# The first chunk's residual accumulated in PSUM by TensorE, its sums copied out by ScalarE

## The chip, the cores and the metric

The kernel runs on one core of one Trainium2 chip. The metric is the device time of one execution in microseconds (us). All times below are of this core; "layer 0" and "layer 1" are the two passes that the program makes over the same pair of stages.

## The reference, cut to what matters

```python
def _A_ref(x, w_r, w_i):                       # spectral filter
    X = rfft2(x.astype(float32), axes=(-2, -1)) * (w_r + 1j * w_i)
    return irfft2(X, s=(S, D)).astype(bfloat16)

def _B_ref(x, w1, b1, w2):                     # dense layer with mish
    h = x @ w1 + b1
    return (h * tanh(softplus(h))) @ w2

x = A_x                                        # bf16, 2048 rows of 1024
for _ in range(2):
    x = x + _A_ref(layernorm(x), A_w_r, A_w_i)
    x = x + _B_ref(layernorm(x), B_w1, B_b1, B_w2)     # F = 3584
```

The place of the change is the seam between the two lines of the loop body: the inverse transform's last step gives sums, the old x is added to them (the residual), each row is normalised (mean and variance over its 1024 values), and the normalised rows enter the first dense product.

## The kernel before, in words

The activations `XS` stay in the on-chip memory SBUF as 16 tiles of 128 rows by 1024 columns. The program is a straight list: every engine (TensorE or PE, VectorE or DVE, ScalarE or ACT, GpSimd or POOL, SyncE or SP) executes its own instructions strictly in the order in which the Python code emits them. Buffers are `Res` objects; an instruction waits for the semaphores of the last writers and readers of what it touches. The accumulator memory PSUM has eight banks of 512 fp32 columns, each with its own `Res`. A matmul group that writes a bank which TensorE itself wrote last waits for TensorE's own semaphore.

`layer_A` is the spectral filter. Its last transform step needs `UT`, which goes through DRAM and comes back by DMA in four quarters (`u_last`). While these are under way, TensorE runs `spin(26, 0)` (L629): 26 matmuls of 512 columns whose results nobody reads, written to bank 0.

`layer_B` begins with that last step, `i4` (L951): for a column l of 128, one matmul with `UT[:, l, :]` as the weights gives sums for some of the 16 tiles. The rows are handled in chunks of four tiles. Chunk 0 (tiles 0 to 3) comes first, in four quarters u of 32 columns of l, quarter u in banks 2u and 2u+1. Per quarter, VectorE adds the sums of tiles 0 and 1 to `XS` in place (L973), ScalarE copies those of tiles 2 and 3 into a staging buffer `YC` (L549), and VectorE takes statistics of the fresh quarter of tiles 0 and 1 (`stats_quarter`, L471, L473). The other twelve tiles are made by `rest(bank, n)`: n columns of l, n matmuls of 96 columns, copied into the staging buffer `YS` by ScalarE, or by VectorE where `dve` is given. In all 128 columns are needed, in pieces of 15, 13 or 10; a piece in bank 3 uses banks 3 to 5, one of ten in bank 6 uses banks 6 and 7.

Then `root` (square root on ScalarE L431, reciprocal on VectorE L433) and `apply` (L511) normalise tiles 0 and 1, `spin(6, 7)` runs, `transposed` turns them by eight TensorE transposes each (L1007) into banks 6 and 7, VectorE copies these out (L1012), and `mm1(chunk, fg, half)` (L1041) is the first dense product, for half a chunk (256 columns) or a whole one (512). ScalarE applies mish (L1045), after a table load (`warm`, L424). Tiles 2 and 3 are added from `YC` (L1117), given statistics (`stats_dve`, L459, L462), scales (L489 to L502) and `apply`, and are turned in the middle of `mm1(0, 3, 0)`.

The order around the change is written out by hand:

```python
for u in range(4):                    # i4, add and copy, stats of quarter u
    ...
rest(0)
self.root(0, 2)
rest(3)
...
for fg in range(4):
    mm1(0, fg, 0, mid=turns(0, 2, 3) if fg == 3 else ())
    rest(3)
    if fg == 2:
        rest(6, 10, dve)
mm1(0, 0, 1)
rest(3, 13)
```

The DMAs of the first weights (`load_w1`) are issued by SP once all of `UT` has landed.

Of the kernel before, what the change touches and what calls it, by code (L numbers as in the profile page):

```python
# [6 lines left out]
ALU = mybir.AluOpType  # L7
P = 128
# [171 lines left out]
class KB:  # L180
# [487 lines left out]
    def layer_A(self, li):  # L668
# [7 lines left out]
        dve, act, sp, pool = self.dve, self.act, self.sp, self.pool  # L676
# [146 lines left out]
        def u_turn(g, half):  # L823

            u = U[g % 3]
            if g == 7:
                h = slice(8 * half, 8 * half + 8)
                if half == 0:
                    u_back(6)
                self.dma(act, self.u_d[g][:, h, :], u.ap[:, h, :], f"uwh{half}", reads=[u.res], writes=[self.r_ud7[half]])  # L830
                if half:
                    u_last()
            elif half:
                self.dma(sp, self.u_d[g], u.ap, f"uw{g % 3}", reads=[u.res], writes=[self.r_ud[g]])
                if g:
                    u_back(g - 1)
# [28 lines left out]
        for stage, g, h in self.order_A():  # L865
# [19 lines left out]
            else:  # L885
                i2(g, h)
                u_turn(g, h)
        self.spin(26, 0)
        if li == 0:
            self.op(self.pool, lambda e: e.tensor_copy(self.B1[:], self.B1h[:]), reads=[self.r_b1h], writes=[self.r_b1])  # L890
        self.w1_buf = [self.alloc(f"W1_{i}", (self.W1_OFF + i * 4096, 140 * K + (i - 4) * 4096)[i > 3], [8, 256]) for i in range(6)]
# [48 lines left out]
    def keep_filter(self, g):  # L940

        i = 2 * g % 8
        self.dma(self.pool, self.w_d[g], self.wt_pair(i), f"ws{g % 4}", reads=[w.res for w in self.WT[i:i + 2]], writes=[self.r_wd[g]])

    def i4(self, lo, nb, u0, n, bank):

        w = 8 * nb
        k = 512 // w
        fns = []
        for l in range(n):  # L950
            fns.append(lambda e, l=l: e.matmul(self.PS[:, bank + l // k, l % k * w:(l % k + 1) * w], self.UT.ap[:, u0 + l, :],  # L951
                                               self.MT[:, 8 * lo:8 * lo + w], start=True, stop=True))
        self.group(fns, reads=self.r_ut[u0 // 32:(u0 + n - 1) // 32 + 1] + [self.r_mt], writes=self.r_bank[bank:bank - (-n // k)])

    def i4_out(self, lo, nb, u0, n, bank, staged=None, prog=None, tiles=None):

        w = 8 * nb
        k = 512 // w
        t0, tn = tiles or (0, nb)

        for b0, m, i in ((0, n // k, k), (n // k, 1, n % k)):
            if not m or not i:
                continue
            src = self.PS[:, bank + b0:bank + b0 + m, 0:i * w].rearrange("p b (i c) -> p c b i", c=w)[:, 8 * t0:8 * (t0 + tn)]
            l = slice(u0 + b0 * k, u0 + b0 * k + m * i)
            rb = self.r_bank[bank + b0:bank + b0 + m]

            def at(ap):
                return ap.rearrange("p n (h l) -> p (n h) l", l=P)[:, :, l].rearrange("p c (b i) -> p c b i", i=i)
            if staged is None:  # L970
                j = slice(lo + t0, lo + t0 + tn)
                xs = at(self.XS[:, j, :])
                self.op(self.dve, lambda e, src=src, xs=xs: e.tensor_tensor(xs, src, xs, ALU.add), reads=rb, parts=self.r_xs[j])  # L973
            else:

                self.copy(prog or self.act, at(staged.ap), src, [], rb, parts=[staged.res])


    def load_w1(self, after=()):
# [7 lines left out]
    def layer_B(self, li, last):  # L987
        pe, dve, act, sp, pool = self.pe, self.dve, self.act, self.sp, self.pool
# [5 lines left out]
        def transposed(c, t, xn, eng=None):  # L994
            bank = 6 + nt[0] % 2
            nt[0] += 1
            xn.unread = False
            if t == 0:
                if XT[c % 2] is None:
                    off = self.ob[f"XT{c % 2}"]  # L1000
                    XT[c % 2] = self.alloc(f"XT{c % 2}", off, [8, 512])
                    r_xt[c % 2] = self.sub_res(XT[c % 2], f"xt{c % 2}h", 2, off, 8192)
                for r in r_xt[c % 2]:
                    r.begin()
            fns = []
            for db in range(8):
                fns.append(lambda e, db=db: e.transpose(PSb[:, bank, db * P:(db + 1) * P], xn.ap[:, db * P:(db + 1) * P],  # L1007
                                                        self.IDENT[:]))
            self.group(fns, reads=[xn.res, self.r_ident], writes=[self.r_bank[bank]])
            dst = XT[c % 2].ap[:, :, t * P:(t + 1) * P]  # L1010
            src = PSb[:, bank, :].rearrange("p (a b) -> p a b", b=P)
            fn = (lambda e: e.activation(dst, src, ACT.Copy)) if eng is act else (lambda e: e.tensor_copy(dst, src))  # L1012
            self.op(eng or dve, fn, reads=[self.r_bank[bank]], parts=[r_xt[c % 2][t // 2]])
# [12 lines left out]
        def mm1(c, fg, half=None, mid=()):  # L1026
            n = base + 14 * (c // 2) + fg
            wb = self.w1_buf[n % 6]
            x = XT[c % 2]
            tok = slice(0, 512) if half is None else slice(256 * half, 256 * half + 256)  # L1030
            w = tok.stop - tok.start
            for fl in range(2):
                if fl:
                    for f in mid:
                        f()
                ft = 2 * fg + fl
                bank = nh[0] % 3
                nh[0] += 1
                fns = []
                for db in range(8):  # L1040
                    fns.append(lambda e, db=db, bank=bank, fl=fl: e.matmul(  # L1041
                        PS[:, bank, 0:w], wb.ap[:, db, fl * P:(fl + 1) * P], x.ap[:, db, tok], start=(db == 0), stop=(db == 7)))
                self.group(fns, reads=[wb.res] + (r_xt[c % 2] if half is None else [r_xt[c % 2][half]]), writes=[self.r_bank[bank]])
                at, ra = AT[c % 2], r_at[c % 2][ft]
                self.op(act, lambda e, bank=bank, ft=ft: e.activation(at.ap[:, ft, tok], PS[:, bank, 0:w], ACT.Mish,  # L1045
                                                                      bias=self.B1[:, ft:ft + 1]),
                        reads=[self.r_bank[bank], self.r_b1], writes=[ra])
            if c % 2 and half != 0 and self.w1_next == n + 6 and n + 6 < base + 28:
                self.load_w1()
# [41 lines left out]

        YS = self.alloc("YS", self.o["YS"], [12, self.D])
        YS.res.begin()
        YC = self.alloc("YC", self.ob["XT1"], [2, self.D])
        YC.res.begin()
        xn = {}
        for j in range(2):
            self.r_xs[j].begin()

        def at_tiles(c):  # L1100
            off = self.ob[f"AT{c}"]
            AT[c] = self.alloc(f"AT{c}", off, [NF, 512])
            r_at[c] = [Res(f"AT{c}_{ft}") for ft in range(NF)]
            for ft, r in enumerate(r_at[c]):
                r.inherit(AT[c].res)
                self.live.append((off + ft * 1024, off + ft * 1024 + 1024, r))

        def rest(bank, n=15, prog=act):

            u0 = self.u0  # L1110
            self.u0 += n
            self.i4(4, 12, u0, n, bank)
            self.i4_out(4, 12, u0, n, bank, staged=YS, prog=prog)

        def residual(j):
            y, i = (YS, j - 4) if j > 3 else (YC, j - 2)
            self.op(dve, lambda e: e.tensor_tensor(self.XS[:, j, :], self.XS[:, j, :], y.ap[:, i, :], ALU.add),  # L1117
                    reads=[y.res], writes=[self.r_xs[j]])

        def turns(c, *ts):  # L1120
            return [lambda t=t: transposed(c, t, xn[4 * c + t]) for t in ts]

        self.u0 = 0


        for u in range(4):
            self.i4(0, 4, 32 * u, 32, 2 * u)
            self.i4_out(0, 4, 32 * u, 32, 2 * u, tiles=(0, 2))
            self.i4_out(0, 4, 32 * u, 32, 2 * u, staged=YC, tiles=(2, 2))
            for j in range(2):  # L1130
                self.stats_quarter(j, u)
        rest(0)
        self.root(0, 2)
        rest(3)
        for j in range(2):
            xn[j] = self.apply(j)
        self.spin(6, 7)
        for j in range(2):
            transposed(0, j, xn[j])
        rest(3)  # L1140
        self.warm(ACT.Mish)
        at_tiles(0)
        for j in (2, 3):
            residual(j)
            self.stats_dve(j)
        self.scales(2, 2)
        for j in (2, 3):
            xn[j] = self.apply(j)
        for fg in range(4):
            mm1(0, fg, 0, mid=turns(0, 2, 3) if fg == 3 else ())  # L1150
            rest(3)
            if fg == 2:
                rest(6, 10, dve)
        mm1(0, 0, 1)
        rest(3, 13)
        assert self.u0 == P
        for j in range(4, 8):
            residual(j)
# [105 lines left out]
```

## Time and profile before

| what | value |
|---|---|
| median of 3 runs | 1017.17 us (1016.41 to 1017.61) |
| profiled execution, its own time | 1017.47 us |
| span of that execution, first to last instruction | 1015.7 us |
| TensorE busy | 959.8 us, 94% |
| VectorE busy | 327.2 us, 32% |
| ScalarE busy | 346.8 us, 34% |
| granted TensorE clock | 1.000 |

The seam of layer 0 lies at 109 to 140 us of the span, that of layer 1 at 600 to 632 us. A TensorE "busy" counts each matmul from its start to its modelled end; as matmuls are pipelined, the step from one to the next is shorter than the duration of one. For sums of TensorE work the step is used: 448 matmuls of 512 columns take 96.69 us in the chain of work, which is 0.2158 us each, and 16 of 256 columns take 1.75 us.

### The profile page before, as it was taken

The numbers are of one execution on the slowest core, as the hardware profiler recorded it, in microseconds if no ns is written. First come the engines' busy times: TensorE is split into PE (matmuls) and PEld (weight loads), VectorE is DVE, ScalarE is ACT, GpSimd is POOL, SyncE is SP. The second block draws the span as 40 slices with busy tenths as digits, with TensorE's granted clock in tenths as the row PEclk, the third lists the DMA queues.
The fourth block names the chain that finished last, engine by engine and source line by source line (L and its number), as shares of the span: only waits on it lengthen the run. The fifth ranks groups of instructions, "written<-read, shape, count | busy, mean of one in ns | idle before, by whom it ended". The sixth has DMA issues, their size and how long they took to land.

```text
span 1015.7 us, 13823 instructions
## 1 busy us (share of the span) xinstructions
PE 959.8 (94%) x5865; PEld 506.5 (50%) x5865; DVE 327.2 (32%) x688; ACT 346.8 (34%) x482; POOL 81.5 (8%) x114
## 2 busy tenths in 40 slices
PE   0799799999999999999999988999999999999998
PEld 0576575444444444444446757644444444444443
DVE  6797469002444000033346736830011100000111
ACT  6898384340000334300019847544100024430000
POOL 3651000000000000002521100000000000000000
PEclk9999999999999999999999999999999999999999
DMA  9979823562111220002922874246411212100000
GB/s 282 245 220 319 212 66 114 178 207 73 47 46 32 73 83 21 1 21 75 206 62 78 237 189 144 85 157 207 127 25 46 74 52 79 46 1 11 21 27 26
DMA packets 154141, 106.99 MB, mean 105 GB/s; under 512 B 74384, under 2 KB 133600, under 8 KB 154080
## 3 DMA queue, kind: packets, MB, share of 16 engines
q1 hardware_dynamic: 143136, 78.88, 27.4%
q0 software_dynamic: 8912, 25.84, 8.8%
q10 hardware_dynamic: 2032, 1.39, 0.5%
q8 instruction: 47, 0.77, 0.3%
q14 instruction: 14, 0.11, 0.0%
HBM read 80.85 MB, written 20.71 MB: 100 GB/s over the span
## 4 chain that ended last, share of the span: by engine, by line
PE 86%; DVE 7%; ACT 3%; DMA 2%; issue 1%; ACTq 0%; POOL 0%; DVEq 0%
PE PS L1058 38%; PE PS L1041 37%; PE PS L772 2%; PE PS L698 2%; PE PS L793 2%; DVE BN L459 1%; DMA ARENA<-c_bt 1%; PE PS L951 1%; DVE ARENA L620 1%; ACT ARENA L549 1%; PE PS L1007 1%; DVE ARENA L593 1%; PE PS L811 1%; ACT ARENA L779 1%; PE PS L629 1%
## 5 line engine op out<-in xcount | busy, mean ns | idle before, releaser
L1041 PE MATMUL PS<-ARENA 128*128 128x512 bf16 (+1 forms) x1984 | 391.1, 358 | 0.7 <-DVE ARENA L1012 0.6
L1058 PE MATMUL PS<-ARENA 128*128 128x512 bf16 x1792 | 387.4, 379 | 0.0
L1045 ACT ACTIVATE ARENA<-PS,B 128x512 bf16<-128x512 f32 (+1 forms) x248 | 158.8, 645 | 411.0 <-PE PS L1041 410.7
L1041 PEld LDWEIGHTS PS<-ARENA 128*128 128x128 bf16 x1984 | 192.8, 98 | 193.8 <-DVE ARENA L1012 1.6
L1058 PEld LDWEIGHTS PS<-ARENA 128*128 128x128 bf16 x1792 | 175.4, 98 | 211.4
L1063 DVE TENSOR_TENSOR XS<-PS,XS 128x512 bf16<-128x512 f32 x64 | 44.3, 692 | 587.0 <-PE PS L1058 587.0
L459 DVE BATCH_NORM_STATS2 BN<-XS 128x6 f32<-128x512 bf16 x100 | 64.7, 676 | 7.5 <-DMA XS<-in_A_x_dram 6.3
L549 ACT ACTIVATE ARENA<-PS 128x1440 bf16<-128x1440 f32 (+3 forms) x26 | 28.0, 1094 | 27.0 <-DVE XS L973 23.3
L249 POOL DMA_DIRECT2D xn_scratch<-ARENA x12 | 6.5, 541 | 374.2 <-DVE ARENA L511 374.2
L772 PE MATMUL PS<-ARENA 128*128 128x256 bf16 x256 | 32.4, 273 | 4.2 <-DVE ARENA L761 3.2
L779 ACT ACTIVATE ARENA<-PS 128x1024 bf16<-128x1024 f32 x32 | 34.0, 1082 | 7.1 <-PE PS L772 7.1
L431 ACT ACTIVATE RS<-MV,EPS 128x2 f32<-128x2 f32 (+2 forms) x5 | 1.5, 298 | 97.5 <-DVE MV L462 96.2
L750 ACT ACTIVATE ARENA<-PS 128x1024 bf16<-128x1024 f32 x32 | 33.2, 1070 | 4.5 <-PE PS L746 4.5
L698 PE MATMUL PS<-FD,ARENA 128*128 128x256 bf16 (+1 forms) x256 | 31.8, 271 | 2.4 <-ACT ARENA L618 1.2
L772 PEld LDWEIGHTS PS<-ARENA 128*128 128x128 bf16 x256 | 24.2, 98 | 11.9 <-DVE ARENA L761 5.6
L754 DVE TENSOR_TENSOR ARENA<-ARENA 128x1024 bf16<-128x1024 bf16 x32 | 22.0, 688 | 21.2 <-ACT ARENA L750 21.2
L821 ACT ACTIVATE ARENA<-PS 128x1024 bf16<-128x1024 f32 x26 | 27.3, 1086 | 2.4 <-PE PS L793 2.4
L698 PEld LDWEIGHTS PS<-FD,ARENA 128*128 128x128 bf16 x256 | 24.4, 98 | 6.5 <-DVE ARENA L620 1.4
L793 PE MATMUL PS<-ARENA,BD 128*128 128x256 bf16 x192 | 24.9, 273 | 2.3 <-ACT ARENA L779 2.3
L511 DVE TENSOR_SCALAR ARENA<-XS,MV,RS 128x1024 bf16<-128x1024 bf16 x48 | 24.9, 543 | 1.0
L733 ACT ACTIVATE ARENA<-PS 128x1024 bf16<-128x1024 f32 x22 | 23.4, 1079 | 3.2 <-PE PS L698 3.2
L951 PE MATMUL PS<-MT,ARENA 128*128 128x32 bf16 (+1 forms) x512 | 20.4, 191 | 4.0 <-ACT ARENA L549 2.5
(76 smaller groups left out, 521.4 us busy)
## 6 DMA issues: line engine op xcount, KB each, us to landing
ARENA<-in_B_w_dram SPq DMA_DIRECT2D x56, 512.0 KB, 3.9
ARENA<-in_B_w_dram SPq DMA_DIRECT2D x56, 256.0 KB, 4.3
u_scratch<-ARENA SPq DMA_DIRECT2D x14, 512.0 KB, 4.7
ARENA<-u_scratch SPq DMA_DIRECT2D x14, 512.0 KB, 6.0
XS<-in_A_x_dram SPq DMA_DIRECT2D x4, 1024.0 KB, 8.7
w_scratch<-ARENA POOLq DMA_DIRECT2D x8, 512.0 KB, 5.9
ARENA<-w_scratch POOLq DMA_DIRECT2D x8, 512.0 KB, 5.1
out_dram<-XS SPq DMA_DIRECT2D x16, 256.0 KB, 2.0
```

The costliest lines, as they stand in the source:

```text
L459: self.op(self.dve, lambda e: e.bn_stats(self.BN[:, j, 6 * h:6 * h + 6], self.XS[:, j, 512 * h:512 * h + 512]), reads=[self.r_xs[j]], part ...
L549: fn = (lambda e: e.activation(dst, src, ACT.Copy)) if scale is None else \
L698: fns.append(lambda e: e.matmul(dst, at(r), FD[:, t:t + n], start=start, stop=stop))
L750: self.op(act, lambda e: e.activation(x.ap.rearrange("p a b -> p (a b)"), ps, ACT.Copy, scale=SIG), reads=banks, writes=[x.res])
L772: fns.append(lambda e, c=c, part=part: e.matmul(ps[:, c * 256:(c + 1) * 256], yk.ap[:, part, c * P:(c + 1) * P], t[:, (128, 0)[part]:(384, ...
L779: self.op(act, lambda e: e.activation(v.ap[:, :, i, :], src, ACT.Copy), reads=banks, parts=[v.res])
L793: fns.append(lambda e, dst=dst, part=part, c=c: e.matmul(dst, BD[:, c:c + P], mov(kd, part), start=(part == 0), stop=(part == 1)))
L951: fns.append(lambda e, l=l: e.matmul(self.PS[:, bank + l // k, l % k * w:(l % k + 1) * w], self.UT.ap[:, u0 + l, :], self.MT[:, 8 * lo:8 * ...
L1041: fns.append(lambda e, db=db, bank=bank, fl=fl: e.matmul(PS[:, bank, 0:w], wb.ap[:, db, fl * P:(fl + 1) * P], x.ap[:, db, tok], start=(db ...
L1045: self.op(act, lambda e, bank=bank, ft=ft: e.activation(at.ap[:, ft, tok], PS[:, bank, 0:w], ACT.Mish, bias=self.B1[:, ft:ft + 1]), reads= ...
L1058: fns.append(lambda e, i=i, ft=ft: e.matmul(PS[:, bank, :], at.ap[:, ft, t * P:(t + 1) * P], W2[ft].ap[:, h * 512:(h + 1) * 512], start=(i ...
L1063: self.op(dve, lambda e: e.tensor_tensor(xs, PS[:, bank, :], xs, ALU.add), reads=[self.r_bank[bank]], writes=[self.r_xs[j]])
```

## The change

- A new function `residual_first` puts x of tiles 0 to 3 into PSUM ahead of the sums: for each of the eight banks one matmul with the identity as weights, whose output lies in the bank with a step of 32 columns. The chunk-0 matmuls of `i4` then accumulate onto it.
- `spin(26, 0)` becomes `spin(18, 0)`, `spin(6, 7)` becomes `spin(4, 7)`.
- `out_first` copies finished sums from PSUM straight into `XS`: tiles 0 and 1 on ScalarE; tiles 2 and 3 after all four quarters, three quarters on ScalarE and the last on VectorE.
- The staging buffer `YC` and the additions of tiles 2 and 3 from it are gone.
- `root` comes ahead of the first two pieces of `rest`. The third piece ahead of `mm1` is gone. In the loop over fg, a piece of 10, 3 and 10 columns goes to bank 6 and VectorE at fg 0, 1 and 2, and the statistics, scales and normalising of tiles 2 and 3 stand after the first of them. The last piece is 15 columns.

```diff
-        self.spin(26, 0)
+        self.spin(18, 0)
...
+    def residual_first(self):
+
+        for b in range(8):
+            out = self.PS[:, b, :].rearrange("p (l c) -> p c l", c=32)
+            xs = self.XS[:, 0:4, :].rearrange("p n (h l) -> p (n h) l", l=P)[:, :, 16 * b:16 * b + 16]
+            self.group([lambda e, out=out, xs=xs: e.matmul(out, self.IDENT[:], xs, start=True, stop=False)],
+                       reads=self.r_xs[0:4] + [self.r_ident], writes=[self.r_bank[b]])
+        for r in self.r_xs[0:4]:
+            r.begin()
...
-                                               self.MT[:, 8 * lo:8 * lo + w], start=True, stop=True))
+                                               self.MT[:, 8 * lo:8 * lo + w], start=lo > 0,
+                                               stop=lo > 0 or l % k == k - 1))
...
+    def out_first(self, u, t, prog):
+
+        b = slice(2 * u, 2 * u + 2)
+        src = self.PS[:, b, :].rearrange("p b (i c) -> p c b i", c=32)[:, 8 * t:8 * t + 16]
+        dst = self.XS[:, t:t + 2, :].rearrange("p n (h l) -> p (n h) l", l=P)[:, :, 32 * u:32 * u + 32]
+
+        self.copy(prog, dst.rearrange("p c (b i) -> p c b i", i=16), src, [], self.r_bank[b], parts=self.r_xs[t:t + 2])
...
+        self.residual_first()
         for u in range(4):
             self.i4(0, 4, 32 * u, 32, 2 * u)
-            self.i4_out(0, 4, 32 * u, 32, 2 * u, tiles=(0, 2))
-            self.i4_out(0, 4, 32 * u, 32, 2 * u, staged=YC, tiles=(2, 2))
+            self.out_first(u, 0, act)
             for j in range(2):
                 self.stats_quarter(j, u)
+        for u in range(4):
+            self.out_first(u, 2, (act, act, act, dve)[u])
+        self.root(0, 2)
         rest(0)
-        self.root(0, 2)
         rest(3)
         for j in range(2):
             xn[j] = self.apply(j)
-        self.spin(6, 7)
+        self.spin(4, 7)
         for j in range(2):
             transposed(0, j, xn[j])
-        rest(3)
         self.warm(ACT.Mish)
         at_tiles(0)
-        for j in (2, 3):
-            residual(j)
-            self.stats_dve(j)
-        self.scales(2, 2)
-        for j in (2, 3):
-            xn[j] = self.apply(j)
         for fg in range(4):
             mm1(0, fg, 0, mid=turns(0, 2, 3) if fg == 3 else ())
             rest(3)
-            if fg == 2:
-                rest(6, 10, dve)
+            if fg < 3:
+                rest(6, (10, 3, 10)[fg], dve)
+            if fg == 0:
+                for j in (2, 3):
+                    self.stats_dve(j)
+                self.scales(2, 2)
+                for j in (2, 3):
+                    xn[j] = self.apply(j)
         mm1(0, 0, 1)
-        rest(3, 13)
+        rest(3)
```

More of the change, by code (lines that the diff above doesn't have):

```diff
@@ L951, in i4, with i4_out @@
             fns.append(lambda e, l=l: e.matmul(self.PS[:, bank + l // k, l % k * w:(l % k + 1) * w], self.UT.ap[:, u0 + l, :],
-                                               self.MT[:, 8 * lo:8 * lo + w], start=True, stop=True))
+                                               self.MT[:, 8 * lo:8 * lo + w], start=lo > 0,
+                                               stop=lo > 0 or l % k == k - 1))
         self.group(fns, reads=self.r_ut[u0 // 32:(u0 + n - 1) // 32 + 1] + [self.r_mt], writes=self.r_bank[bank:bank - (-n // k)])
-    def i4_out(self, lo, nb, u0, n, bank, staged=None, prog=None, tiles=None):
+    def out_first(self, u, t, prog):
[3 more added lines that the diff above has]
+        self.copy(prog, dst.rearrange("p c (b i) -> p c b i", i=16), src, [], self.r_bank[b], parts=self.r_xs[t:t + 2])
+    def i4_out(self, lo, nb, u0, n, bank, staged, prog):
         w = 8 * nb
         k = 512 // w
-        t0, tn = tiles or (0, nb)
         for b0, m, i in ((0, n // k, k), (n // k, 1, n % k)):
@@ L963, in i4_out @@
                 continue
-            src = self.PS[:, bank + b0:bank + b0 + m, 0:i * w].rearrange("p b (i c) -> p c b i", c=w)[:, 8 * t0:8 * (t0 + tn)]
+            src = self.PS[:, bank + b0:bank + b0 + m, 0:i * w].rearrange("p b (i c) -> p c b i", c=w)
             l = slice(u0 + b0 * k, u0 + b0 * k + m * i)
[L966 to L976, printed above, removed]
+            dst = staged.ap.rearrange("p n (h l) -> p (n h) l", l=P)[:, :, l].rearrange("p c (b i) -> p c b i", i=i)
+            self.copy(prog, dst, src, [], self.r_bank[bank + b0:bank + b0 + m], parts=[staged.res])
     def load_w1(self, after=()):
@@ L1093, in layer_B @@
         YS.res.begin()
-        YC = self.alloc("YC", self.ob["XT1"], [2, self.D])
-        YC.res.begin()
         xn = {}
-        for j in range(2):
-            self.r_xs[j].begin()
         def at_tiles(c):
@@ L1115, in residual @@
         def residual(j):
-            y, i = (YS, j - 4) if j > 3 else (YC, j - 2)
-            self.op(dve, lambda e: e.tensor_tensor(self.XS[:, j, :], self.XS[:, j, :], y.ap[:, i, :], ALU.add),
-                    reads=[y.res], writes=[self.r_xs[j]])
+            self.op(dve, lambda e: e.tensor_tensor(self.XS[:, j, :], self.XS[:, j, :], YS.ap[:, j - 4, :], ALU.add),
+                    reads=[YS.res], writes=[self.r_xs[j]])
         def turns(c, *ts):
```

## The prediction

> **What bounds the kernel now.** I read the page's first part, the chain that ended last in order of time, and then each engine's timeline over the two seams.
>
> ```profile
> PE 959.8 (94%) x5865; PEld 506.5 (50%) x5865; DVE 327.2 (32%) x688; ACT 346.8 (34%) x482; POOL 81.5 (8%) x114
> ...
> PE 86%; DVE 7%; ACT 3%; DMA 2%; issue 1%; ACTq 0%; POOL 0%; DVEq 0%
> ```
>
> TensorE is the bound; all else counts only where TensorE waits. The seam of layer 1 in the chain:
>
> ```profile
> 602.31 4.20 DMA ARENA<-u_scratch
> 606.65 0.96 PE PS L951 x32
> 607.64 0.70 DVE XS L973
> 608.37 0.75 DVE BN L471 x2
> ...
> 611.88 0.60 DVE XS L973
> 612.50 1.86 ACT ARENA L549 x2
> 614.36 0.19 ACT RS L431
> 614.78 0.56 DVE ARENA L511
> 615.38 1.08 PE PS L1007 x16
> ```
>
> One quarter of sums is made in 0.96 us. Then VectorE carries four rounds of add and statistics, about 1.375 us each. ScalarE follows with the last copy and the first copy of the rest (1.86 us together), and only then comes its square root. On TensorE:
>
> ```profile
> 600.05 5.79 PE L629 MATMUL PS<-FD,BD 128*128 128x512 bf16 x26 [1.33 <-DVE ARENA L819]
> 606.65 3.35 PE L951 MATMUL PS<-MT,ARENA 128*128 128x32 bf16 x128 [0.81 <-DMA ARENA<-u_scratch]
> ...
> 613.15 1.47 PE L629 MATMUL PS<-FD,BD 128*128 128x512 bf16 x6 [0.57 <-ACT ARENA L549]
> 615.38 1.08 PE L1007 MATMUL PS<-IDENT,ARENA 128*128 128x128 bf16 x16 [0.76 <-DVE ARENA L511]
> ```
>
> I count time from the first sum matmul (606.65 is t = 0). The first dense matmul is at 617.38, t = 10.73; the one behind the last piece of `rest` is at 631.94, t = 25.29. Layer 0 has 115.03 and 140.32, again 25.29. The steps of TensorE between: `mm1` fg 0 to 3 of 16 matmuls each, 7.00; turning tiles 2 and 3, 1.08; `mm1(0,0,1)`, 1.75; 83 columns of `rest` at 0.0427 (15 take 0.64 in the chain), 3.54. That is 13.37, so 25.29 - 10.73 - 13.37 = 1.19 us are waits. Behind t = 25.29 TensorE is dense to the layer's end, so what t = 25.29 becomes goes one to one into the time, twice.
>
> [...] this trace has accumulation at the plain pace (0.2158 a step in L1058). [...]
>
> **The change part by part.**
>
> **1. Residual in, spins out.** Removed: eight spin matmuls of 0.2158, 1.73 us, per layer. Added: eight residual matmuls. The step of one lies between 0.2158 (the same 512 columns; [...] every row of 512 columns steps so) and four times that. I take twice, 0.43[...]. Reading XS in runs of 16 costs nothing: L922 reads in runs of four and has 275 ns against 273. The first residual writes bank 0 behind the spin and waits for its end: layer 0 shows that as 115.03 - (108.93 + 26 x 0.2158) = 0.49. Before, the sums waited the same 0.49.
> Layer 0: 108.93 + 18 x 0.2158 + 0.49 + 8 x 0.43 = 116.7 against 115.03, so +1.7 (0 at the plain pace, +5.2 at four times).
> Layer 1: 600.05 + 3.88 + 0.49 + 3.44 = 607.9 against 606.65, where the DMA of `UT` set the start, so +1.2 (0 at the plain pace, since the DMA covers 0.5; +4.7 at four times).
> No DMA is moved, on any queue; SP's weight loads are released by `UT` as before.
>
> **2. The front.** ScalarE copies quarter u of tiles 0 and 1 in 0.60 (the L549 row of 512 columns has 597 ns). Quarters are ready every 0.82 us, so copies end at t = 1.6, 2.4, 3.2, 4.0. VectorE has only statistics: the last pair with its two aggregates takes 1.3 (612.50 to 613.81), to 5.3; before, 7.15. Then VectorE's copy of the last quarter of tiles 2 and 3, 0.65, to 6.0. ScalarE does the other three at 0.5 to 0.6, to 5.6; square root 0.30, reciprocal 0.17, `apply` 0.5: tile 0 is normalised at 6.8 instead of 8.7.
> TensorE meanwhile: `rest(0)` waits for banks 0 to 2, 5.1 to 5.8; `rest(3)` for banks 3 to 5, 5.8 to 6.5; four spins to 7.4; so the transposes start at 7.4 and not at 6.8, then 2.0 to the first dense matmul (615.38 to 617.38): **t = 9.4 instead of 10.73**, a gain of 1.3. ScalarE copies the two rests to 8.8, its table load ends at 10.3 and the first mish can start at 10.45: covered, as no bank is wanted before.
>
> **3. The moved piece of rest.** Before, 15 columns lay between transposes and dense product, hidden behind VectorE's copies. Now 98 columns come after it instead of 83: +0.64. The removed adds from `YC`, two of 0.64 to 0.68 on VectorE, lay beside TensorE: worth nothing directly, but see 4.
>
> **4. The wait that comes instead.** Tiles 2 and 3 used to be treated right behind the copies of the first transposes:
>
> ```profile
> 617.24 0.68 DVE L1117 TENSOR_TENSOR XS<-XS,ARENA 128x1024 bf16<-128x1024 bf16 x1
> 617.96 1.29 DVE L459 BATCH_NORM_STATS2 BN<-XS 128x6 f32<-128x512 bf16 x2
> ...
> 623.23 1.00 DVE L511 TENSOR_SCALAR ARENA<-XS,MV,RS 128x1024 bf16<-128x1024 bf16 x2
> 626.01 1.16 DVE L553 CAST ARENA<-PS 128x960 bf16<-128x960 f32 x1 [1.78 <-PE PS L951]
> ```
>
> They ended at 624.23, so bank 6 was free long before its piece. Now VectorE idles from 9.4 until the ten columns of fg 0 are made (t = 9.4 + 1.74 + 0.64 + 0.43 = 12.2) and has behind one another: their copy 1.16, statistics of two tiles 2.9 (636.09 to 639.00 for tiles 4 and 5), scales 1.6 (639.04 to 640.58), two `apply` 1.0, and only then the copy of fg 1's three columns, 0.45. With two hand-overs of 0.1 each that is 7.3 us. The piece of fg 2 writes bank 6 again and waits for it. Until there TensorE has `mm1(0,1)` 1.74, 15 columns 0.64, three columns 0.13, `mm1(0,2)` 1.74, 15 columns 0.64: 4.9. **TensorE waits 2.4 us**, and queued behind this wait is all of `mm1(0,3)`. Then the turns wait 0.5 for the copy of that piece, as before (0.38 and its issue). ScalarE, with a piece each fg, keeps up: it frees bank 3 about 0.3 before each piece. The W1 blocks have a median of 6.6 us to land, 608.22 + 6.6 = 614.8, ahead of 616.
>
> **Sum per layer:** 9.4 + (7.00 + 1.08 + 1.75 + 98 x 0.0427 = 14.0) + 2.4 + 0.5 = 26.3 against 25.29, +1.0. With the start: layer 0 +2.7, layer 1 +2.2, together **+4.9 us**. The profiled execution took 1017.47, which is 1.8 around its span and 0.3 over the median; 1017.47 + 4.9 = 1022.4, and for a median as before **1022.0**.
>
> **The rivals.**
>
> *The residual matmuls run at the plain pace.* [...] Then only the +1.0 per layer is left, and up to 0.3 in layer 0, whose last quarter of sums ends at t = 3.9 and not 3.4: +2.2, **1019.4**. Chance 25%.
>
> *They run at a quarter of it.* [...] +5.2 + 4.7 + 2.0 gives **1029.0**. Chance 8%.
>
> *The wait for bank 6 does not arise*, so that the head start stays: VectorE's queue between fg 0 and fg 2 would be at or below 4.9 us instead of 7.3. [...] Against: every row is measured in the same order elsewhere in this trace. Then t = 9.4 + 14.0 + 0.5 = 23.9, 1.4 less per layer, and at the plain pace **1014.4**. It turns the sign, at the plain pace, once the queue is shorter than 6.3. Chance 7%.
>
> *The additions only change engine and the front doesn't move*, because ScalarE with seven copies ahead of the square root takes VectorE's place. From the rows: four copies end at 4.0 and three more take at most 1.8, so it costs 0.3 at most; it lies in the range.
>
> **How the numbers follow.** My forecast has 60% and by itself runs from 1020.8 to 1023.5. With the plain pace below and some of the slower case above, the range is **1018.0 to 1026.0**. About 0.2%, 2 us, is what a measurement of this kernel can tell from no change. Slower by more: 60 + 8 + half of the plain-pace case, 80%. Within it: the other half, 13%. Faster: 7%.
>
> **What would show it.** Residual matmuls stepping at 0.43 and the first sums 1.7 and 1.2 later in the two layers; transposes 7.4 after the first sums and the dense product 9.4; a TensorE wait of about 2.4 us for VectorE's copy of 288 elements, in each layer, ahead of a piece of ten columns; the dense product behind the last piece 26.3 after the first sums. No such wait, or residuals below 0.25 apart, would make the forecast wrong.

## The result, and the profile after

The changed kernel takes 1025.91 us in the median of 4 runs (1024.48 to 1026.84), the kernel before 1017.39 on the same chip. The ratio is **1.0081, 95% interval 1.0062 to 1.0099**: slower by 0.8%. The profiled execution is the quickest of the four, 1024.48 us, with a span of 1022.7 against 1015.7.

The page's busy times and the chain by engine, after:

```profile
PE 958.4 (94%) x5775; PEld 508.8 (50%) x5861; DVE 324.3 (32%) x682; ACT 348.4 (34%) x484; POOL 81.6 (8%) x114
...
PE 86%; DVE 8%; ACT 2%; DMA 2%; issue 1%; ACTq 0%; POOL 0%; DVEq 0%
```

The shares tell nothing: TensorE has 1.4 us less busy time in the records (some matmul records are missing, 5775 of 5861), and the span is 7.0 longer. The difference lies in the two seams, which are 3.79 and 3.30 us longer (measured as under "The experiments"). Time line of layer 1 after the change (columns: start, busy us, engine, line, operation, tiles, shape, count, and in brackets the idle time before and what ended it). `residual_first` is L950, the sums and rests are L961, the turns L1016, the dense product L1050. The first of the 18 spins has no record; it is taken to start one step of 0.2158 before the second, at 108.84 in layer 0 and 603.76 in layer 1:

```profile
603.97 3.83 PE L629 MATMUL PS<-FD,BD 128*128 128x512 bf16 x17 [1.55 <-DVE ARENA L819]
607.87 3.61 PE L950 MATMUL PS<-XS,IDENT 128*128 128x512 bf16 x8
611.27 3.40 PE L961 MATMUL PS<-MT,ARENA 128*128 128x32 bf16 x128
616.33 1.45 PE L961 MATMUL PS<-MT,ARENA 128*128 128x96 bf16 x30 [1.67 <-ACT XS L549]
...
618.48 1.06 PE L1016 MATMUL PS<-IDENT,ARENA 128*128 128x128 bf16 x16
...
620.47 1.92 PE L1050 MATMUL PS<-ARENA 128*128 128x256 bf16 x16 [0.94 <-DVE ARENA L1021]
...
629.09 1.00 DVE L511 TENSOR_SCALAR ARENA<-XS,MV,RS 128x1024 bf16<-128x1024 bf16 x2
630.01 0.79 DVE L553 CAST ARENA<-PS 128x288 bf16<-128x288 f32 x1
630.85 0.60 PE L961 MATMUL PS<-MT,ARENA 128*128 128x96 bf16 x10 [2.50 <-DVE ARENA L553]
...
632.71 1.89 PE L1016 MATMUL PS<-IDENT,ARENA 128*128 128x128 bf16 x16 [0.38 <-DVE ARENA L553]
...
634.38 1.71 PE L1050 MATMUL PS<-ARENA 128*128 128x256 bf16 x8
```

Eight residual matmuls take the time from 607.87 to the first sums at 611.27, 0.43 us each. The first dense product is 9.20 us behind the first sums (10.73 before). At 630.85 stands the wait for bank 6, ended by VectorE's copy of 288 elements that came directly behind the two `apply` at 629.09. And then something new: the turns take 1.67 us to the next instruction (0.90 at the same place before), the half product behind them 1.55 (0.87). The windows over that stretch give the reason. They are cut where the clock changes; the column after the bracketed busy times is the granted TensorE clock:

```profile
core 0: us, PE busy (x) PEld busy (x) DVE busy (x) ACT busy (x) POOL busy (x), PEclk, DMA share, GB/s
628.91:632.33 3.42, 1.47 (x18) 1.12 (x18) 2.69 (x5) 0.85 (x1) 0.00 (x0) 1.00 0.00 0
632.33:635.74 3.41, 3.04 (x23) 2.67 (x24) 1.70 (x3) 0.47 (x1) 0.00 (x0) 0.50 0.02 5
```

TensorE is busy for 1.47 of 3.42 us, and for the next 3.41 its clock is 0.50. Layer 0 has the same, with clock 0.50 from 137.39 to 140.81.

### The profile page after: what moved, and what is told of

Same layout as the page of the kernel before. It is cut to its first block, busy times and chain, and to the rows that moved or that the text cites. A ratio compares the mean times of both kernels' runs of the same rounds, so it can differ in the third digit from the quotient of the medians.

```text
span 1022.7 us, 13729 instructions
## 1 busy us (share of the span) xinstructions
PE 958.4 (94%) x5775; PEld 508.8 (50%) x5861; DVE 324.3 (32%) x682; ACT 348.4 (34%) x484; POOL 81.6 (8%) x114
## 4 chain that ended last, share of the span: by engine, by line
PE 86%; DVE 8%; ACT 2%; DMA 2%; issue 1%; ACTq 0%; POOL 0%; DVEq 0%
PE PS L1067 38%; PE PS L1050 37%; PE PS L772 2%; PE PS L698 2%; DVE BN L459 2%; PE PS L793 2%; PE PS L961 1%; PE PS L629 1%; DMA ARENA<-c_bt 1%; DVE ARENA L620 1%; PE PS L1016 1%; PE PS L950 1%; DVE ARENA L593 1%; PE PS L811 1%; DVE ARENA L553 1%
## 5 line engine op out<-in xcount | busy, mean ns | idle before, releaser
L1050 PE MATMUL PS<-ARENA 128*128 128x512 bf16 (+1 forms) x1950 | 390.4, 359 | 3.8 <-DVE ARENA L1021 1.9
L1050 PEld LDWEIGHTS PS<-ARENA 128*128 128x128 bf16 x1984 | 193.8, 98 | 195.3 <-DVE ARENA L1021 2.9
L772 PEld LDWEIGHTS PS<-ARENA 128*128 128x128 bf16 x256 | 24.0, 98 | 12.1 <-DVE ARENA L761 5.7
L961 PE MATMUL PS<-MT,ARENA 128*128 128x32 bf16 (+1 forms) x512 | 20.0, 191 | 8.3 <-DVE ARENA L553 5.0
L961 PEld LDWEIGHTS PS<-MT,ARENA 128*128 128x128 bf16 x512 | 18.8, 97 | 10.3 <-DVE ARENA L553 5.3
```

The lines of the kernel that those rows point to most:

```text
L772: fns.append(lambda e, c=c, part=part: e.matmul(ps[:, c * 256:(c + 1) * 256], yk.ap[:, part, c * P:(c + 1) * P], t[:, (128, 0)[part]:(384, ...
L1050: fns.append(lambda e, db=db, bank=bank, fl=fl: e.matmul(PS[:, bank, 0:w], wb.ap[:, db, fl * P:(fl + 1) * P], x.ap[:, db, tok], start=(db ...
```

## The experiments

All ratios are to the kernel before, run on the same chip, with 95% intervals. "Half clock" below is a stretch of 3.41 us, or two or three such stretches in a row, in which the granted clock is 0.50. (Wider windows, and windows that straddle a change, show a mean above 0.50.) To compare seams whatever came before them, I give the time from the first spin to the first dense matmul behind the last piece of `rest`: before 31.39 us in layer 0 and 31.89 in layer 1, after 35.18 and 35.19.

### Ten spins in the wait: e1_fill

```diff
             rest(3)
+            if fg == 2:
+                self.spin(10, 7)
             if fg < 3:
```

> The changed kernel with ten spin matmuls (2.16 us) put into TensorE's 2.5 us wait ahead of the ten-column piece of fg 2; nothing else changes. Theory A (the wait costs twice: 2.5 us of standing still, and behind it some 3 us at a little over half clock, which stretches the turns and half a dense product by 1.3 us per layer): the piece starts when it did, no slice falls below clock 1.00, the eight dense matmuls behind the turns take 0.87 instead of 1.55, and the time falls by 2.6 us or somewhat more against the changed kernel, to 5 to 6 us above the kernel before. Theory B (the turns and the product are slow there because ScalarE and VectorE disturb them, or for another reason that has nothing to do with the wait): no difference, 7 to 8.5 us above.

Measured: 1023.40 us, ratio 1.0061 (1.0048 to 1.0073), against 1.0081 for the change. The ten columns start where they did, 10.4 us behind the first dense product; the turns and the half product run at full pace in both layers. Windows of layer 1:

```profile
626.00:630.00 4.00, 4.00 (x41) 2.91 (x39) 3.65 (x14) 3.65 (x4) 0.00 (x0) 1.00 0.00 0
630.00:634.00 4.00, 3.27 (x40) 2.38 (x39) 2.59 (x4) 0.47 (x1) 0.00 (x0) 1.00 0.01 4
```

VectorE and ScalarE do the same work there as in the changed kernel, so theory B falls. The full pace in the trace is what shows this; the two intervals of the ratio overlap a little. But layer 1 now has half clock at another place, between sums and turns (0.60 from 614 to 618), and the first dense product comes 10.75 behind the first sums instead of 9.20.

### Five spins in the wait: e7_fill5

The same line with `self.spin(5, 7)`.

> The changed kernel with five spin matmuls (1.08 us) in the 2.5 us wait of TensorE, so that some 1.4 us of it are left. Theory A (the clock falls when too little is done over some microseconds; 1.4 us stand still between dense stretches in the kernel before as well, without a fall): no half clock behind the wait in either layer, time as with ten spins, 1023 to 1024. Theory B (any wait of over a microsecond there brings it): half clock stays and so does the time of the changed kernel, 1025 to 1026.

Measured: 1024.84 us, ratio 1.0064 (1.0051 to 1.0077). A wait of 1.44 us is left in each layer, and no half clock stands behind it: theory A for this place. The time came out a microsecond above the expectation, since both layers of the profiled execution have half clock between sums and turns (in layer 1 a mean of 0.81 and 0.76 in the two windows of 4 us from 614).

### The old order, with the residual in PSUM: e2_oldorder

```diff
             transposed(0, j, xn[j])
+        rest(3)
         self.warm(ACT.Mish)
         at_tiles(0)
+        for j in (2, 3):
+            self.stats_dve(j)
+        self.scales(2, 2)
+        for j in (2, 3):
+            xn[j] = self.apply(j)
         for fg in range(4):
...
-            if fg < 3:
-                rest(6, (10, 3, 10)[fg], dve)
-            if fg == 0:
-                for j in (2, 3):
-                    self.stats_dve(j)
-                self.scales(2, 2)
-                for j in (2, 3):
-                    xn[j] = self.apply(j)
+            if fg == 2:
+                rest(6, 10, dve)
         mm1(0, 0, 1)
-        rest(3)
+        rest(3, 13)
```

> The changed kernel with its residual in PSUM and its copies kept, but with the order of before put back from the transposes on: a third piece of rest ahead of the table load, statistics and normalising of tiles 2 and 3 straight behind the first transposes, one piece of ten columns at fg 2, a last piece of 13. Theory A (the loss is in the order: bank 6 taken three times with the statistics in between): no wait of over 1 us for VectorE's copy, no half clock, the product behind the last piece about 24.2 us after the first sums (27.7 in the changed kernel, 25.3 before); what is left of the loss is the later start, 1.3 and 0.9 us, and the front gives about as much back: 1 us below to 1 us above the kernel before. Theory B (accumulating on the residual and copying by ScalarE costs within the seam): over 4 us above before.

Measured: 1018.82 us, ratio 1.0009 (1.0000 to 1.0017). Of the waits for a rest copied by VectorE only the 0.38 of before is left. In layer 1 the product behind the last piece is 24.33 after the first sums, as expected. In layer 0 it is 25.39, because half clock again lies between sums and turns there. So nearly the whole loss is in the order. Accumulating and copying cost nothing that shows beyond the later start and this half clock.

### Fewer spins ahead: e3_spin10

```diff
-        self.spin(18, 0)
+        self.spin(10, 0)
```

> The changed kernel with 10 spin matmuls instead of 18 ahead of the residual, which takes out the time by which eight stepped residual matmuls (0.43 us each) exceed eight plain ones. Theory A (TensorE itself makes the first sums late): first sums 1.3 us earlier against the last copy of U in layer 0 and 0.9 us in layer 1, where the returning transform data then set the start again; the time falls by about 2.2 us. Theory B (the start is set by the arrival of the data or by the copies of the banks in front): no change of the start, no change of the time.

Measured: 1025.61 us, ratio 1.0076 (1.0063 to 1.0089): no gain that shows. The start did move, as theory A had it, though less in layer 1. Layer 0:

```profile
109.03 2.33 PE L629 MATMUL PS<-FD,BD 128*128 128x512 bf16 x10 [1.32 <-DVE ARENA L819]
111.42 3.61 PE L950 MATMUL PS<-XS,IDENT 128*128 128x512 bf16 x8
114.82 1.00 PE L961 MATMUL PS<-MT,ARENA 128*128 128x32 bf16 x32
116.15 2.55 PE L961 MATMUL PS<-MT,ARENA 128*128 128x32 bf16 x96 [0.33 <-DMA ARENA<-u_scratch]
120.37 1.79 PE L961 MATMUL PS<-MT,ARENA 128*128 128x96 bf16 x30 [1.67 <-ACT XS L549]
123.65 1.57 PE L1016 MATMUL PS<-IDENT,ARENA 128*128 128x128 bf16 x16
```

The rests begin 11.3 behind the first spin instead of 12.6, and the second quarter now waits for its data. In layer 1 it is 12.1 instead of 12.6. But from there to the dense product it takes 5.7 and 5.6 us in the two layers instead of 4.1: half clock in both. What the earlier start gave, 1.2 and 0.5 us, the clock took, and more.

### The step on the reading side: e4_contig

```diff
-            out = self.PS[:, b, :].rearrange("p (l c) -> p c l", c=32)
-            xs = self.XS[:, 0:4, :].rearrange("p n (h l) -> p (n h) l", l=P)[:, :, 16 * b:16 * b + 16]
+            out = self.PS[:, b, :].rearrange("p (l c) -> p l c", c=32)
+            xs = self.XS[:, 0:4, :].rearrange("p n (h l) -> p l (n h)", l=P)[:, 16 * b:16 * b + 16, :]
```

> The changed kernel with the two patterns of the residual matmul swapped: PSUM is written in order, x is read with a step of 128 elements (256 bytes) from one element to the next. Theory A (the step in PSUM is what halves the rate): residual matmuls step at 0.216 us, the first sums come 1.3 to 1.7 us earlier in layer 0 and 0.9 in layer 1, time 2.2 us below the changed kernel. Theory B (scattered elements cost as much on the reading side): 0.43 us a step or more, no gain, or a loss if it is more.

Measured: 1033.51 us, ratio 1.0155 (1.0141 to 1.0169). Residual and sums of layer 0:

```profile
114.67 7.03 PE L950 MATMUL PS<-XS,IDENT 128*128 128x512 bf16 x8
121.52 3.60 PE L961 MATMUL PS<-MT,ARENA 128*128 128x32 bf16 x128
```

(121.52 - 114.67) / 8 = 0.856 us each, four times the plain pace. Theory B, and more than it said: with a step of 256 bytes from element to element of the operand that is read, a matmul takes twice the 0.43 that it takes with the step in PSUM. Half clock begins while these matmuls run, in both layers (at 119.21 in layer 0); their step is 0.86 before and after it begins.

### The layout in the bank turned: e6_turned and e5_turned_old

`cols` takes the place of the slice of columns in `i4`'s output.

```diff
-            out = self.PS[:, b, :].rearrange("p (l c) -> p c l", c=32)
+            out = self.PS[:, b, :].rearrange("p (c l) -> p c l", l=16)
...
+            cols = slice(l % k * w, (l % k + 1) * w) if lo else slice(l % k, 512, k)
...
-        src = self.PS[:, b, :].rearrange("p b (i c) -> p c b i", c=32)[:, 8 * t:8 * t + 16]
+        src = self.PS[:, b, :].rearrange("p b (c i) -> p c b i", i=16)[:, 8 * t:8 * t + 16]
```

With the order of the change:

> The changed kernel with its own order and only the layout within a bank turned, as above: the step moves from the 512-column residual to the 32-column sums. Theory A: residual at 0.216, first sums 1.7 us earlier in layer 0 (or as soon as the data are there) and 0.9 in layer 1; the wait for bank 6 and the half clock behind it stay as they are; against the changed kernel 2.2 us less, and up to 1.5 less again in the executions in which a second stretch of half clock lies between sums and turns, if that one comes from the half-rate residual: 1021.5 to 1023.5. Theory B (the second stretch comes from the waits at the banks, not from the residual): it stays, and 1023.5 to 1025.5 is measured.

Measured: 1022.92 us, ratio 1.0057 (1.0040 to 1.0073). Residual matmuls step at 0.216, and half clock between sums and turns is gone from both layers, as theory A forecast. That this comes from the residual is not shown, since the sums are stepped now as well (see below). Behind the wait for bank 6 the clock is halved in layer 1 and, with the same wait of 2.52, at 1.00 throughout in layer 0, on which see below.

With the old order:

> The residual in PSUM, the copies and the order of before from the transposes on, as in the run with the old order, and the layout within a bank turned: the residual matmul writes 512 columns in order and reads runs of 16, while each 32-column matmul of the sums writes with a step of 16 columns. Theory A (the stepped write costs only where it exceeds what a matmul takes anyway: 32 columns at half rate are 27 ns, and these step at 26 ns; the residual goes to 0.216; the sums start when they did in the kernel before; TensorE is dense ahead of them, so no half clock): 1.0 us per layer faster than before by the seam alone, about 2 us in all, 1015 to 1016. Theory B (the step costs the narrow matmul as much as it did the wide one, in time and not in rate, or half clock comes at this place whatever stands ahead): the same as the old order, 1018 to 1019, or slower.

Measured: 1018.48 us, ratio 1.0002 (0.9995 to 1.0010). Layer 1:

```profile
602.43 4.06 PE L629 MATMUL PS<-FD,BD 128*128 128x512 bf16 x18 [1.32 <-DVE ARENA L819]
606.55 1.90 PE L950 MATMUL PS<-XS,IDENT 128*128 128x512 bf16 x8
608.59 3.89 PE L962 MATMUL PS<-MT,ARENA 128*128 128x32 bf16 x128
```

The residual is at the plain pace, but the 128 narrow matmuls take 3.89 us instead of 3.35: stepped writes are not free for them, 0.5 us per layer. This seam takes 30.99, 0.9 under before. In layer 0 the returning data came 1.7 later than TensorE was ready for them, and the seam takes 32.56. The 2 us that theory A expected did not appear in the time.

### Pairs of columns: e9_pairs

```diff
-            out = self.PS[:, b, :].rearrange("p (l c) -> p c l", c=32)
+            out = self.PS[:, b, :].rearrange("p (g c t) -> p c g t", c=32, t=2)
...
+            g0 = l % k // 2 * 64
+            cols = slice(l % k * w, (l % k + 1) * w) if lo else slice(g0 + l % 2, g0 + 64, 2)
...
-        src = self.PS[:, b, :].rearrange("p b (i c) -> p c b i", c=32)[:, 8 * t:8 * t + 16]
+        src = self.PS[:, b, :].rearrange("p b (g c t) -> p c (b g) t", c=32, t=2)[:, 8 * t:8 * t + 16]
```

x and `XS` are split into the same pairs, and the order is the old one.

> The run with the old order and the residual in PSUM, with a third layout within a bank: the residual matmul writes runs of two fp32, with 64 columns from one run to the next, and reads runs of 16; the 32-column matmuls of the sums write with a step of two columns. Theory A [...]: residual matmuls 0.216 us apart although their output is scattered, sums at 0.029 us a matmul as in the turned layout; time as with that, 1017 to 1019. Theory B (any write that is not in order over the whole bank halves the rate): 0.43 us apart as in the changed kernel, 1018.5 to 1020.5.

Measured: 1017.38 us, ratio 0.9999 (0.9988 to 1.0009). Layer 1:

```profile
605.10 1.90 PE L951 MATMUL PS<-XS,IDENT 128*128 128x512 bf16 x8
606.95 3.89 PE L964 MATMUL PS<-MT,ARENA 128*128 128x32 bf16 x128
```

Eight matmuls whose output jumps by 64 columns behind every second value: 1.90 us, the plain pace. The sums at 0.029, although their step is only two columns. Theory A on both. The seams take 31.00 and 30.79, 0.4 and 1.1 under before, in the one execution profiled; the time does not show it.

### The square root ahead, in the kernel before: e8_before_root

```diff
-        rest(0)
         self.root(0, 2)
+        rest(0)
         rest(3)
```

> The kernel before with one line moved: the square root stands ahead of the first piece of rest, as in the changed kernel; nothing else is changed. Theory A (the head start of 1.5 us at the first dense product comes from taking the add off VectorE, and the order of the root gives little): the square root 0.3 us earlier at most in each layer, the dense product 0.2 to 0.3 earlier, time 0 to 0.6 us below the kernel before. Theory B (the root's place behind a copy of 1440 elements is what held the front): over 1 us per layer, 1015.

Measured: 1019.05 us, ratio 1.0010 (1.0002 to 1.0017). The seams take 31.65 and 31.82, so the order of the root brings nothing: turns start 8.50 instead of 8.73 behind the first sums in layer 1, and then TensorE waits 0.74 for ScalarE's copy of a rest. Why the time is 0.1% longer I don't know.

### TensorE left idle, in the kernel before: e10_idle

```diff
-        self.spin(26, 0)
+        self.spin(6, 0)
```

> The kernel before with 6 spin matmuls instead of 26 ahead of the first sums, so that TensorE stands still for some 4.5 us there; no residual in PSUM, order and copies as before. Theory A (half clock follows a stretch in which TensorE did too little, and needs neither the stepped residual nor the wait for bank 6): in both layers a stretch of about 3.4 us with the clock near 0.5 over the first sums, rests and turns; the 32-column sums are not slower for it, the rests and turns are; 0.5 to 1.5 us per layer, 1019 to 1021. Theory B (half clock in the changed kernel came from the stepped writes or the bank waits as such): full clock in both seams and the time of the kernel before.

Measured: 1019.24 us, ratio 1.0014 (1.0008 to 1.0021). TensorE stands still for 4.0 and 6.4 us ahead of the sums. Layer 1:

```profile
602.00:606.00 4.00, 0.00 (x0) 0.00 (x0) 0.00 (x0) 0.00 (x0) 0.00 (x0) 1.00 0.24 60
606.00:610.00 4.00, 1.67 (x63) 1.70 (x64) 0.62 (x1) 0.00 (x0) 0.00 (x0) 0.55 0.43 85
610.00:614.00 4.00, 3.71 (x99) 3.45 (x96) 3.90 (x10) 1.79 (x3) 0.00 (x0) 0.59 0.72 210
```

Theory A: neither the step nor bank 6 is needed for half clock. These waits are longer than the 2.5 us of the changed kernel, so they say nothing of how short a wait suffices. All 21 runs of this kernel have a mean clock of 0.991 to 0.995.

## Why the prediction was right, and where it was short

The sign, the place and the range (1018.0 to 1026.0) held, the range by 0.1 us at 1025.91, and that was luck: its upper part stood there for a residual at a quarter of the pace, which did not come, and half clock, which no term foresaw, filled it. The size did not hold: +4.9 us was forecast, and the profiled executions stand 7.0 apart, the medians 8.5. Term by term, in us per layer, from the two profiled executions:

| step of the prediction | forecast | measured |
|---|---|---|
| 1. start of the sums, layer 0 / layer 1 | +1.7 / +1.2 | +1.4 / +0.9 |
| 2. head start to the dense product | -1.3 | -1.5 |
| 3. moved piece of rest | +0.64 | +0.64 |
| 4. waits in the dense product, less those of before | +1.7 | +1.8 |
| half clock behind the wait | not in the sum | +1.4 |
| sum, layer 0 / layer 1 | +2.7 / +2.2 | +3.8 / +3.3 |

In the sum itself, the turns of tiles 2 and 3 stand with 1.08 us, which is their duration; their step is 0.90 (before, layer 1: 627.23 to 628.13). With that, as with the steps of the other terms, the forecast would have been about 0.2 us per layer lower.

**Step 1.** The stepped residual at 0.43 was the choice among three values, and it is what was measured (3.40 / 8). For such a step all three were estimates of mine: no matmul of the trace of before writes with one. The rivals at 0.216 and 0.86 fall for this layout. The start came 0.3 less late because the residual waits only 0.23 for the spins ahead of it (112.95 against 108.84 + 18 x 0.2158), not the 0.49 that the sums waited. In e8_before_root the sums too wait only 0.24 behind 26 spins, in both layers, so the 0.49 was not the price of that wait alone. In e9_pairs runs of two step at 0.216, in the changed kernel runs of one at 0.43. The output of e9_pairs is scattered too, it jumps by 64 columns behind every second value, and that costs the residual nothing. What halves the pace of single values is not shown.

**Step 2.** The dense product came 9.20 behind the first sums, for 9.4. So the front moved, and the rival in which it does not is out. ScalarE is what TensorE waits for there now: the first rest starts 5.06 behind the first sums, after a wait of 1.67 for ScalarE's copies, close to the forecast of 5.1. The place of the square root gave none of this (e8_before_root).

**Step 4.** The wait for bank 6 was 2.50 for 2.4, from VectorE's queue as listed; the copy of three columns took 0.79, not 0.45, and what stands ahead of it in the queue 6.52 (623.49 to 630.01) for 6.9, so two errors offset each other. e2_oldorder shows that this order is the loss: with the old one the ratio goes from 1.0081 to 1.0009. The rival in which the wait does not arise is out.

**The step that failed is the price of the wait.** The prediction counted a microsecond of waiting as a microsecond. TensorE's clock was not in the sum; the kernel before gave no hint of it, with a mean of 1.000. The eight seams with an unfilled wait of 2.5 us (after, e3, e4 and e6, two layers each) have half clock behind it in seven cases. The four in which spins left 0.35 or 1.44 us have none. Half clock costs 1.4 us there: 1.67 - 0.90 for the turns and 1.55 - 0.87 for the product.

Why one of the eight escaped can be read from the clock. Within each profile, its changes in the span lie whole multiples of 3.41 us apart (137.39 and 632.33 in the changed kernel, 145 times 3.413), so the trace can be cut into such stretches. The wait of e6_turned in layer 0, 133.08 to 135.60, has a boundary in its middle, 134.34:

```profile
130.92:134.34 3.42, 2.16 (x29) 1.86 (x27) 3.07 (x13) 3.19 (x4) 0.00 (x0) 1.00 0.00 0
134.34:137.75 3.41, 1.77 (x24) 1.43 (x25) 2.36 (x4) 0.62 (x2) 0.00 (x0) 1.00 0.00 0
```

TensorE is busy for 2.16 and 1.77 us of the two stretches. In the seven stretches ahead of a fall it is 0.90 to 1.52 us (1.47 in the lines shown for the changed kernel), with five spins 1.98 in both layers and no fall. So what counts, as far as these cases show, is how much work is left in such a stretch; the wait that escaped has 1.26 us on either side of a boundary, that of the changed kernel in layer 1 (628.35 to 630.85) 0.56 ahead of one and 1.94 behind. This is no sharp limit: in e10_idle a stretch with 1.47 us of spins is not followed by a fall.

A second effect of the same kind probably makes the medians differ by more than the profiled pair. Of the 12 seams with residual matmuls at half pace or less, 8 have half clock ahead of the turns: both of e3 and e7 and one each of e1 and e2 between sums and turns, where it costs 1.5 to 1.6 us, and both of e4, where it begins during the residual. The two of after have none, and none of the 10 with the plain pace or no residual (before, e5, e6, e8, e9). The other three timed executions of the changed kernel, 1025.64 to 1026.84, have a mean clock of 0.993 to 0.995 against 0.996 in the profiled one, which fits such stretches; without profiles of them that is an inference.

From 8 and 10 one might conclude that a matmul at half pace counts as half idle. The stretches speak against it. In layer 1 of e7_fill5 the last residual matmul gives way to the sums at 611.45:

```profile
613.11:616.52 3.41, 1.74 (x71) 1.64 (x67) 3.23 (x9) 2.83 (x6) 0.00 (x0) 1.00 0.95 279
616.52:619.93 3.41, 3.41 (x33) 2.82 (x34) 1.88 (x6) 2.63 (x4) 0.00 (x0) 0.50 1.10 319
```

The stretch ahead of the fall holds sums, the wait for ScalarE's copies and (in e2 and layer 0 of e3 and e7) the first rests, but no residual matmul. So it is in all six cases of e1, e2, e3 and e7 (1.74 to 2.05 us busy). A stretch that is residual at half pace to all but 0.05 us, 113.01 to 116.42 in e1_fill, has full clock behind it; one that is all residual at a quarter of the pace, 115.79 to 119.21 in e4_contig, has half clock. A narrow matmul in order may count for less than its time: an estimate is that its 32 columns need 0.0135 us (0.2158 / 16) of the 0.025 from one to the next. The narrow matmuls of e5, e6 and e9, at 0.029, have a stepped output, and no fall follows there, not even with 2.12 us busy (e6_turned, 117.27 to 120.68) where e3_spin10 falls with 2.05 (612.83 to 616.24). No run tests this, nor that only the last stretch counts; the cause of the second effect stays open, and what sets the clock is not shown.

No version tried beats the kernel before by more than the measurement can tell. e9_pairs and e5_turned_old have shorter seams in three of the four of their profiles, and the same time. The wait for the data of `UT`, 1.71 us in layer 0 of e5, and half clock ahead of the seams, which the profiles of e5 and e9 show and mean clocks of 0.995 to 0.998 in many runs of the kernel before suggest, are as large as what is left to gain.

## What to carry to other kernels

Price a new wait of the bounding engine twice: once for its length, and once for the clock that it may lose behind it; here 2.5 us of waiting cost 1.4 more, and idle matmuls put into the wait took that back at this place without shortening it. A single profile without half clock does not show that the wait is safe, since it depends on where the boundaries of the stretches fall in it: in e6_turned the same wait of 2.5 us left full clock in layer 0, with a boundary in its middle, and half clock in layer 1. When buffers are handed round more often, look at what the engine that frees them has to do between one use and the next: three uses of bank 6 with 5.4 us of statistics and normalising between them cost more than the whole front had gained. Before moving an addition into PSUM, look which of the two patterns is stepped, and by how much: here a matmul took 0.43 us with single values in the output, 0.856 with them in the operand that is read, and 0.216 with runs of two in the output.

## What the runs showed of the hardware that was not expected

- A matmul of 512 columns, on record for 0.379 us (L1058 before), steps at 0.216 us with its output in order or in runs of two fp32 (e6_turned, e9_pairs), at 0.43 with single fp32 a step of 32 columns apart (the changed kernel), and at 0.856 when it reads single bf16 values 256 bytes apart (e4_contig, at clock 1.00 and 0.50 alike).
- A matmul of 32 columns, which steps at 0.025 us in order (before), steps at 0.029 when its output has a step of 2 (e9_pairs) or of 16 columns (e5_turned_old).
- A wait of 2.5 us on TensorE between dense stretches was followed by 3.41 us at half clock in seven of eight cases, waits of 0.35 and 1.44 us at the same place in none of four. Matmuls of 32 columns hardly show it (0.027 us from one to the next in e10_idle instead of 0.025), those of 96 columns do (0.080 in layer 1 of e1_fill instead of 0.043).
- Within each profile the granted clock changes only at whole multiples of 3.41 us from one another, wherever the program stands (in the changed kernel at 137.39, 140.81, 632.33 and 635.74).
